# One decode step of attention and a gated feed-forward on one core: Gate's weights loaded in pieces of 112, 8 and 8 rows

## The chip, the cores and the metric

The kernel runs on one core of a Trainium2 chip. The metric is the device time of one execution in microseconds (us), as a median over repeated executions. Profiles are one execution each, taken by the hardware profiler; TensorE is called PE there (PEld for its weight loads), VectorE DVE, ScalarE ACT, GpSimd POOL and SyncE SP (SPq where it issues transfers).

## What is computed

One token (a row of 640 numbers) goes through a block with conditioning: a layer norm with a scale and a shift, attention over a cache of 16384 positions in 32 heads of 128, a gate and a residual; then a second layer norm, a gated feed-forward of width 1728, a gate and a residual. The reference, cut:

```python
mod = (_silu(c) @ w_mod).reshape(c.shape[0], 6, 1, -1)     # sa, ca, ga, sb, cb, gb
h = _layernorm(x) * (1 + ca) + sa
x = x + ga * attention(h, A_k_cache, A_v_cache, A_wq, A_wo)
h = _layernorm(x) * (1 + cb) + sb
x = x + gb * ((_silu(h @ w_gate) * (h @ w_up)) @ w_down)
```

All arrays are bf16. The two caches are 128 MiB each; `w_gate` and `w_up` are 640 x 1728 and `w_down` is 1728 x 640, some 2.2 MB each.

## The kernel before, in words

The caches go through the core once. Heads are taken in pairs, sixteen of them (`NP`). K of a pair (8 MB) goes to one of the two halves of `kring`, V to `vbuf`. The scores are made on VectorE: it multiplies K by the query laid out over the partitions (lines 546 and 561) and folds the products (lines 550, 555 and 567); TensorE adds up the rest with the identity as weights (lines 537 and 575). Softmax runs on ScalarE (line 593), and TensorE multiplies V by the weights (line 493). In the last pair (lines 639 to 647) K comes in two pieces and V in four, so that the work behind the last bytes is short.

Nearly all transfers are issued by SyncE, in the order in which the program lists them, through the helper at line 80. Each is issued when the buffer that it overwrites is free. Towards the end the order is: K of the last pair, V of the last pair but one, the output projection `A_wo` (into the half of `kring` that is free by then), V of the last pair in four pieces, and then the weights of the feed-forward, into the other half of `kring` (`kb`): gate (`wg_v`), up in two pieces (`wu_v`), down in four (`wd_v`). These last seven all wait for one thing, `o_R[NP - 1]`, the last sum of the scores on TensorE (line 704), which ends at about 640 us. So all of them stand in the queue behind V's last pieces, and each engine that moves data takes its share of one after the other.

Gate's load (line 705) is a single one. `w_gate` is laid out so that partition p holds five consecutive rows of the matrix: 5 x 1728 x 2 = 17280 bytes in a partition, one packet of the trace each, 128 in all. Here "row" means such a packet: the share of one partition. A load of 128 rows is moved by sixteen DMA engines, eight rows each, and each engine adds to the load's semaphore when its share has landed.

What uses these weights, on TensorE in this order: `gate0` (line 761) multiplies the first fifth of the gate matrix by `ab`, which VectorE makes from the second layer norm (line 759); then come the sum for the variance (line 381), the rest of gate (line 767), the residual as rows (`x1_rows`, line 780), `up0` and `up1` (lines 782 and 783) and, when VectorE has made `gu` (line 791) from both, the four parts of the down projection, `down0` to `down3` (line 805, matmuls at line 802). Each of the four waits for its own load (wd0 to wd3), and wd3 has only 96 rows, of 2560 bytes. VectorE then applies the last gate and the residual (lines 806 and 807), and the output is stored.

In the plan, every operation has a list of those that it depends on (`deps`), every load a semaphore of its own, and an engine waits for each semaphore with one instruction of its own ahead of the operation (lines 133 to 138).

Of the kernel before, what the change touches and what calls it, by code (L numbers as in the profile page):

```python
# [37 lines left out]
class _Plan:  # L38
# [28 lines left out]
    def op(self, eng, fn, deps=(), name="", chan=None):  # L67
        o = _Op(eng, fn, list(deps), name, len(self.ops), self.loop.get(eng), chan)
        o.sig = chan is not None
        self.ops.append(o)  # L70
        return o

    def dma(self, out_ap, in_ap, key, deps=(), name="", eng="sp", noncontig=False):
        nc = self.nc

        def fn(e, out_ap=out_ap, in_ap=in_ap, noncontig=noncontig):
            if noncontig:
                with nc.allow_non_contiguous_dma(reason="tiny vector layout change"):
                    return e.dma_start(out_ap, in_ap)
            return e.dma_start(out_ap, in_ap)  # L80

        return self.op(eng, fn, deps, name, chan=self.dma_chan(key))
# [125 lines left out]
def build(nc, A_x, A_k, A_v, A_wq, A_wo, B_wg, B_wu, B_wd, c_in, w_mod, out):  # L208
# [21 lines left out]
    with es:  # L230
        block = es.enter_context(nc.Block())
        plan = _Plan(nc, es)
        op, dma = plan.op, plan.dma
        POOL, ACT, DVE, PE = "pool", "act", "dve", "pe"
# [12 lines left out]
        wg_v = kb[:, 0:KC * F].rearrange("p (k n) -> p k n", k=KC)  # L247
# [68 lines left out]
        g_ps = psb[0]  # L316
# [53 lines left out]
        def layernorm_ops(src_f32, src_dep, sum_ap, c0, tag, xc_t, free=None, between=None):  # L370
            st_ps = misc
            o_tot = op(PE, lambda e: e.matmul(st_ps[:, c0:c0 + 1], lhsT=ones_f[:], rhs=sum_ap, start=True, stop=True),
                       deps=[src_dep, o_onesf, free], name=tag + "_tot")
            o_xc = op(DVE, lambda e: e.scalar_tensor_tensor(
                out=xc_t[:], in0=src_f32[:], scalar=float(D), in1=st_ps[:, c0:c0 + 1].broadcast_to([128, KC]),
                op0=ALU.mult, op1=ALU.subtract), deps=[o_tot, src_dep], name=tag + "_xc")
            o_sq = op(ACT, lambda e: e.activation(
                out=junk[:], in_=xc_t[:], func=ACTF.Square, accum_out=st[:, c0 + 1:c0 + 2]), deps=[o_xc], name=tag + "_sq")
            if between:
                between(o_xc)  # L380
            o_tot2 = op(PE, lambda e: e.matmul(st_ps[:, c0 + 1:c0 + 2], lhsT=ones_f[:], rhs=st[:, c0 + 1:c0 + 2], start=True, stop=True),
                        deps=[o_sq], name=tag + "_tot2")
            o_ln = op(ACT, lambda e: e.activation(
                out=st[:, c0 + 2:c0 + 3], in_=st_ps[:, c0 + 1:c0 + 2], func=ACTF.Ln, scale=1.0 / float(D) ** 3, bias=EPS),
                deps=[o_tot2], name=tag + "_ln")
            o_rstd = op(ACT, lambda e: e.activation(
                out=st[:, c0 + 3:c0 + 4], in_=st[:, c0 + 2:c0 + 3], func=ACTF.Exp, scale=-0.5, bias=-math.log(float(D))),
                deps=[o_ln], name=tag + "_rstd")
            return o_xc, o_rstd
# [20 lines left out]
        def f_mod(e, m0, m1):  # L410
# [11 lines left out]
            deps=[o_mod, o_xn], name="t1")  # L422
# [23 lines left out]
        for g in range(H // 4):  # L446
            b = g % 2
# [9 lines left out]
            for half in range(2):  # L457
# [4 lines left out]
                    deps=[o_q[g]], name="qbc%d_%d" % (g, half)))  # L462
# [54 lines left out]
        def diag_last():  # L517

            p, last = NP - 1, o_diag[NP - 2]
            copies = [op(ACT, lambda e, h=h: e.activation(  # L520
                out=acc_sb[:, 256 * h:256 * h + 256], in_=acc_ps[:, 256 * h:256 * h + 256], func=ACTF.Copy),
                deps=[o_pv[p], last], name="acc%d_%d" % (p, h)) for h in range(2)]
            for h in range(2):
                def f_diag(e, h=h):
                    out = None
                    for i in (2 * h, 2 * h + 1):
                        out = e.matmul(OT_ps[:, 0:2], lhsT=acc_sb[:, 128 * i:128 * (i + 1)], rhs=sel[:, i:8:4],  # L527
                                       start=(i == 0), stop=(i == 3))
                    return out
                o_diag[p] = op(PE, f_diag, deps=[copies[h], o_sel, o_ot[p - 1]], name="diag%d_%d" % (p, h))  # L530
            return o_diag[p]
# [89 lines left out]
        a = 0  # L621
        while a < len(GROUPS):
            b = a
            while b < len(GROUPS) and GROUPS[b][1] == GROUPS[a][1]:
                b += 1
            (h0, n), h1 = GROUPS[a], GROUPS[b - 1][0] + GROUPS[b - 1][1]
            d = dma(wo_v[:, h0:h1, :].rearrange("p (g k) n -> p g (k n)", k=n),
                    A_wo[h0 * 128:h1 * 128, :].rearrange("(g p k) n -> p g (k n)", p=128, k=n),
                    ("wo", a), deps=[o_R[NP - 2]], name="dma_wo%d" % a)
            for i in range(a, b):  # L630
                d_wo[i] = d
            a = b
# [12 lines left out]
                  deps=[o_exp[PL - 1], o_rz, o_onesf, o_rstd], name="La")  # L645
# [4 lines left out]
                  deps=[o_rla] + o_ot[0:NP - 1], name="on")  # L650
# [31 lines left out]
        def project(g):  # L682
            h0, n = GROUPS[g]

            def f_wo(e):
                last = None
                for k in range(h0, h0 + n):
# [11 lines left out]
                  deps=[o_exp[PL], o_rla], name="Lb")  # L699
# [2 lines left out]


        wdeps = [o_R[NP - 1]]
        d_wg = dma(wg_v, B_wg.rearrange("(p k) n -> p k n", p=128), "wg", deps=wdeps, name="dma_wg")
        wu_src = B_wu.rearrange("(p k) n -> p k n", p=128)
        UK = KC - 1
        d_wu = [dma(wu_v[:, 0:UK, :], wu_src[:, 0:UK, :], "wu0", deps=wdeps, name="dma_wu0"),
# [10 lines left out]
        for g in range(NG):  # L719
# [3 lines left out]
                   deps=[o_rl, diag_last()], name="on_last")  # L723

        def f_wol(e):
# [10 lines left out]
        o_zg = op(DVE, lambda e: e.memset(g_ps[:, 0:2 * FCH], 0.0), deps=[o_exp[NP - 2]], name="zero_g")  # L736
# [5 lines left out]
            deps=[o_ga, o_xf], name="x1")  # L742

        def chunk(j):
            return (slice(512 * (j // 4) + j % 4, 512 * (j // 4) + 512, 4), 128) if j < 4 * NB else (slice(512 * NB + j % 4, F, 2), FR)

        def f_gu(e, wv, ps_t, src, n, k0, k1):
            last = None
            for k in range(k0, k1):
                for j in range(FCH):  # L750
                    cols, w = chunk(j)
                    last = e.matmul(ps_t[0:w, n * j:n * j + n], lhsT=wv[:, k, cols], rhs=src[:, n * k:n * k + n],
                                    start=(k == 0 and j == 0), stop=(k == KC - 1 and j == FCH - 1), skip_group_check=True)
            return last
        ab_f = ab[:].rearrange("p k n -> p (k n)")
        o_g0 = []

        def gate0(o_xc1):
            o_a = op(DVE, lambda e: e.tensor_tensor(out=ab[:, :, 0], in0=xc1[:], in1=onep_b[:], op=ALU.mult),
                     deps=[o_xc1, o_onep_b, o_abs], name="ab_a")  # L760
            o_g0.append(op(PE, lambda e: f_gu(e, wg_v, g_ps, ab_f, 2, 0, 1), deps=[o_a, d_wg, o_zg], name="gate0"))
        o_xc1, o_rstd1 = layernorm_ops(x1, o_x1, st[:, 4:5], 4, "ln2", xc1, o_rl, gate0)
        o_t2 = op(DVE, lambda e: e.scalar_tensor_tensor(
            out=tt3[:], in0=xc1[:], scalar=st[:, 7:8], in1=onep_b[:], op0=ALU.mult, op1=ALU.mult),
            deps=[o_xc1, o_rstd1, o_onep_b], name="t2")
# [48 lines left out]
def bass_adaLN_cond__gqa_block_cached__swiglu_ffn__decode_kernel(  # L814
    nc: bass.Bass,
    A_x: bass.AP,
    A_k_cache: bass.AP,
    A_v_cache: bass.AP,
    A_wq: bass.AP,
    A_wo: bass.AP,  # L820
    B_x: bass.AP,
    B_w_gate: bass.AP,
    B_w_up: bass.AP,
    B_w_down: bass.AP,
    c: bass.AP,
    w_mod: bass.AP,
    out: bass.AP,
):
    build(nc, A_x, A_k_cache, A_v_cache, A_wq, A_wo, B_w_gate, B_w_up, B_w_down, c, w_mod, out)
# [28 lines left out]
```

## Time and profile before

| What | Value |
|---|---|
| median of 3 runs | 682.11 us (682.03 to 682.45) |
| the profiled execution: time | 682.26 us |
| the profiled execution: span of the profile | 680.5 us |
| data moved | 290.63 MB, mean 427 GB/s over the span |
| VectorE busy | 512.4 us (75%) |
| TensorE busy | 372.1 us (55%) |
| gate's load: issue, from issue to landing | 640.62 us, 25.2 us |
| down's loads: issue, from issue to landing | 641.94 us on, 30.6 to 33.5 us |

The span begins with the first instruction and ends with the last; the profiled execution's time holds 1.8 us more around it. Start times below are in us from the span's start. A line of the timeline gives start, duration, engine, line of the program, operation, what is written and read, the number of instructions and, in brackets, how long the engine had been idle and what released it. The chain of waits is followed back from the last instruction: each piece is what released the one after it. Beside instructions and packets, the trace keeps the time of every addition to a semaphore, and so of the sixteen arrivals of each load, though not the name of the engine that made one.

### The profile page before, as it was taken

Reading aid. Unit: us, or ns where it says so; the run is one execution under the profiler, and the core shown is the slowest. Engines: PE = TensorE matmul, PEld = TensorE weight load, DVE = VectorE, ACT = ScalarE, POOL = GpSimd, SP = SyncE. Lnnn points to the kernel's source line nnn. Section 1 sums busy time; section 2 is a strip of 40 time slices with the busy share of each in tenths; the row PEclk is TensorE's granted clock in tenths of the full one; section 3 lists DMA queues with packets and bytes.
Section 4 is the critical chain, followed back from the end, with each engine's and each line's share of the span. In section 5 each row is a group of like instructions: output and inputs, shape, how many; then the busy total and the mean of one; then the engine's idle time right before and its main releaser. Section 6 shows DMA issues by size and latency. Waiting matters only on the chain.

```text
span 680.5 us, 5104 instructions
## 1 busy us (share of the span) xinstructions
PE 372.1 (55%) x2271; PEld 151.9 (22%) x2272; DVE 512.4 (75%) x191; ACT 46.0 (7%) x146; POOL 0.7 (0%) x6
## 2 busy tenths in 40 slices
PE   2532275756638184655728275664817375572866
PEld 2311122221212122221302122221202122131435
DVE  2079998959596986959597895959598795999402
ACT  1120000100000000100000000000000010000100
POOL 0000000000000000000000000000000000000000
PEclk9975565655756565565657565565757555575665
DMA  8999999999999999999999999999999999999996
GB/s 369 443 460 429 431 431 428 432 432 431 431 431 431 431 435 431 435 431 435 431 431 431 431 447 443 439 435 435 431 431 431 431 431 431 410 453 403 436 414 271
DMA packets 7575, 290.63 MB, mean 427 GB/s; under 512 B 810, under 2 KB 1068, under 8 KB 2060
## 3 DMA queue, kind: packets, MB, share of 16 engines
q1 hardware_dynamic: 7560, 290.48, 99.1%
q8 instruction: 8, 0.13, 0.1%
q14 instruction: 3, 0.02, 0.0%
q10 hardware_dynamic: 4, 0.00, 0.0%
HBM read 290.47 MB, written 0.00 MB: 427 GB/s over the span
## 4 chain that ended last, share of the span: by engine, by line
DMA 54%; DVE 35%; PE 10%; SPq 0%; issue 0%; ACT 0%
DMA kring<-in_A_k_cache_dram 44%; DVE kring L546 17%; DVE kring L550 8%; PE psb L537 7%; DMA kring<-in_B_w_down_dram 5%; DMA vbuf<-in_A_v_cache_dram 4%; DVE kring L555 4%; DVE kring L561 3%; DVE kring L567 2%; PE psb L493 2%; PE psb L575 1%; SPq L80 0%; DVE pm L581 0%; PE psb L802 0%; PE psb L510 0%
## 5 line engine op out<-in xcount | busy, mean ns | idle before, releaser
L546 DVE TENSOR_TENSOR kring<-kring,qbc 128x16384 bf16<-128x16384 bf16 x28 | 243.3, 8688 | 95.1 <-DMA kring<-in_A_k_cache_dram 95.1
L537 PE MATMUL psb<-kring,ident 128*128 128x256 bf16 x448 | 197.4, 607 | 118.6 <-DVE kring L555 118.6
L550 DVE TENSOR_TENSOR kring<-kring 128x8192 bf16<-128x8192 bf16 x28 | 123.8, 4420 | 0.5
L537 PEld LDWEIGHTS psb<-kring,ident 128*128 128x128 bf16 x448 | 51.8, 121 | 248.5 <-DVE kring L555 128.3
L493 PE MATMUL psb<-vbuf,PZ 128*8 128x512 bf16 x1024 | 90.1, 526 | 11.4 <-DMA vbuf<-in_A_v_cache_dram 11.3
L585 PE MATMUL psb<-d,bd_f 128*128 128x64 f32 x32 | 11.0, 447 | 113.8 <-ACT d L583 113.8
L555 DVE TENSOR_TENSOR kring<-kring 128x4096 bf16<-128x4096 bf16 x28 | 64.0, 2286 | 0.5
L561 DVE TENSOR_TENSOR kring<-kring,qbc 128x16384 bf16<-128x16384 bf16 x4 | 34.7, 8687 | 17.0 <-DMA kring<-in_A_k_cache_dram 17.0
L493 PEld LDWEIGHTS psb<-vbuf,PZ 128*8 128x8 bf16 x1024 | 28.5, 109 | 77.2 <-issue 61.7
L585 PEld LDWEIGHTS psb<-d,bd_f 128*128 128x128 f32 x32 | 8.0, 311 | 115.6 <-DVE pm L581 58.2
L575 PE MATMUL psb<-kring,ident 128*128 128x128 bf16 x64 | 14.5, 393 | 35.0 <-DVE kring L567 35.0
L567 DVE TENSOR_TENSOR kring<-kring 128x8192 bf16<-128x8192 bf16 (+2 forms) x12 | 31.7, 2645 | 0.3
L510 PEld LDWEIGHTS psb<-sel,acc_sb 128*128 128x128 f32 x120 | 27.5, 318 | 7.2 <-issue 4.3
L510 PE MATMUL psb<-sel,acc_sb 128*128 128x2 f32 x120 | 24.5, 326 | 0.7 <-ACT acc_sb L501 0.7
L501 ACT ACTIVATE acc_sb<-psb 128x512 f32<-128x512 f32 x15 | 9.0, 597 | 209.7 <-PE psb L493 209.7
L593 ACT ACTIVATE PZ<-psb,nb 64x256 bf16<-64x256 f32 x32 | 15.0, 469 | 63.0 <-DVE nb L589 62.8
L575 PEld LDWEIGHTS psb<-kring,ident 128*128 128x128 bf16 x64 | 7.5, 122 | 41.4 <-DVE kring L567 36.1
L452 PE MATMUL psb<-vbuf,h_col 128*128 128x512 bf16 x39 | 11.0, 453 | 7.9 <-DMA vbuf<-in_A_wq_dram 7.9
L722 DVE TENSOR_TENSOR A_sb<-psb,rl 128x2 bf16<-128x2 f32 x1 | 0.2, 159 | 19.7 <-PE psb L527 19.7
L583 ACT ACTIVATE d<-negid,pm 128x64 f32<-128x64 f32 x16 | 5.6, 348 | 138.3 <-DVE pm L581 138.0
L514 ACT ACTIVATE OT_sb<-psb 128x2 f32<-128x2 f32 x15 | 2.6, 172 | 153.1 <-PE psb L510 153.1
L581 DVE TENSOR_REDUCE pm<-psb 128x1 f32<-128x256 f32 x16 | 6.7, 418 | 1.8 <-PE psb L575 1.8
(103 smaller groups left out, 91.6 us busy)
## 6 DMA issues: line engine op xcount, KB each, us to landing
kring<-in_A_k_cache_dram SPq DMA_DIRECT2D x4, 4096.0 KB, 37.6
vbuf<-in_A_wq_dram SPq DMA_DIRECT2D x1, 5120.0 KB, 27.0
kring<-in_w_mod_dram SPq DMA_DIRECT2D x1, 4800.0 KB, 14.1
vbuf<-in_A_v_cache_dram SPq DMA_DIRECT2D x1, 4096.0 KB, 15.7
kring<-in_A_wo_dram SPq DMA_DIRECT2D x1, 3840.0 KB, 29.2
kring<-in_B_w_gate_dram SPq DMA_DIRECT2D x1, 2160.0 KB, 25.2
vbuf<-in_A_v_cache_dram SPq DMA_DIRECT2D x1, 2048.0 KB, 20.2
kring<-in_B_w_down_dram SPq DMA_DIRECT2D x3, 640.0 KB, 32.3
```

Of the source, the lines that this page charges most:

```text
L452: last = e.matmul(q_ps[b][:, 0:512], lhsT=h_col[:, k:k + 1].broadcast_to([128, 128]), rhs=wq_v[:, k, g * 512:(g + 1) * 512], start=(k == 0 ...
L493: last = e.matmul(acc_ps[32 * s:32 * s + 8, :], lhsT=PZ[:, p % 2, j, :], rhs=vbuf[:, 4 * j:4 * j + 4, :].rearrange("p t d -> p (t d)"), st ...
L510: last = e.matmul(OT_ps[:, 0:2], lhsT=acc_sb[:, 128 * i:128 * (i + 1)], rhs=sel[:, i:8:4], start=(i == 0), stop=(i == 3))
L537: last = e.matmul(S_ps[p % 2][:, 0:T2], lhsT=ident[:], rhs=kring[:, p % 2, :, d], start=(d == 0), stop=(d == QW + QR - 1))
L546: o_m = op(DVE, lambda e: e.tensor_tensor(out=kv4, in0=kv4, in1=q4, op=ALU.mult), deps=[d_k[p][-1]] + o_qev[p // 2], name="mult%d_%d" % (p ...
L550: o_f = op(DVE, lambda e: e.tensor_tensor(out=kv4[:, :, 0], in0=kv4[:, :, 0], in1=kv4[:, :, 1], op=ALU.add), deps=[o_m], name="fold%d_%d" ...
L555: return op(DVE, lambda e: e.tensor_tensor(out=lo[:, :, 0:QR], in0=lo[:, :, 0:QR], in1=lo[:, :, QR:QW], op=ALU.add), deps=[o_f], name="fol ...
L561: o = op(DVE, lambda e: e.tensor_tensor(out=kv, in0=kv, in1=qbc[:, p, :].unsqueeze(1).broadcast_to([128, KCUT[c + 1] - KCUT[c], 128]), op= ...
L567: o = op(DVE, lambda e, w=w: e.tensor_tensor(out=kv[:, :, 0:w], in0=kv[:, :, 0:w], in1=kv[:, :, w:2 * w], op=ALU.add), deps=[o], name="fol ...
L575: last = e.matmul(S_ps[p % 2][:, KCUT[c]:KCUT[c + 1]], lhsT=ident[:], rhs=kring[:, p % 2, KCUT[c]:KCUT[c + 1], d], start=(d == 0), stop=(d ...
L585: o_mx[p] = op(PE, lambda e: e.matmul(mx_ps[:, 0:64], lhsT=bd_f[:], rhs=d2[:], start=True, stop=True), deps=[o_d2, o_bd1, o_bd2, o_nb[p - ...
L593: o_exp[p] = op(ACT, lambda e, half=half, ps=ps: e.activation(out=PZ[ps, p % 2, :, 4 * half:4 * half + 4], in_=S_ps[p % 2][ps, 0:T2].rearr ...
```

## The change

The single load of gate's weights becomes three: rows 0 to 111, rows 112 to 119 and rows 120 to 127. They are issued one after the other at the place of the old one, each with a semaphore of its own, and `gate0` waits for all three. 112 rows are seven for each of sixteen engines; the two loads of eight rows are meant for one row on each of the lower eight engines, so that these move nine rows and the upper eight seven. The same bytes go to the same places.

```diff
         wdeps = [o_R[NP - 1]]
-        d_wg = dma(wg_v, B_wg.rearrange("(p k) n -> p k n", p=128), "wg", deps=wdeps, name="dma_wg")
+        wg_src = B_wg.rearrange("(p k) n -> p k n", p=128)
+        d_wg = [dma(wg_v[a:b], wg_src[a:b], ("wg", a), deps=wdeps, name="dma_wg%d" % a) for a, b in ((0, 112), (112, 120), (120, 128))]
         wu_src = B_wu.rearrange("(p k) n -> p k n", p=128)
...
-            o_g0.append(op(PE, lambda e: f_gu(e, wg_v, g_ps, ab_f, 2, 0, 1), deps=[o_a, d_wg, o_zg], name="gate0"))
+            o_g0.append(op(PE, lambda e: f_gu(e, wg_v, g_ps, ab_f, 2, 0, 1), deps=[o_a, o_zg] + d_wg, name="gate0"))
```

## Prediction

> **What bounds the kernel now.** I read the page first, then the windows of the last 40 us, the timeline of the end, the chain and the waits. From the page:
>
> ```profile
> span 680.5 us, 5104 instructions
> ...
> DMA  8999999999999999999999999999999999999996
> ...
> q8 instruction: 8, 0.13, 0.1%
> q14 instruction: 3, 0.02, 0.0%
> ```
>
> The transfers are busy from the second slice to the last but one: the kernel moves 290.63 MB at a mean of 427 GB/s and waits for little else. The two last lines look idle, but they matter below: code loads of 16 KB and 8 KB run on the same sixteen DMA engines. The windows of the tail (columns: busy time of PE, PEld, DVE, ACT and POOL, then PEclk, DMA share, GB/s):
>
> ```profile
> 660.00:665.00 5.00, 3.95 (x34) 2.38 (x22) 0.30 (x4) 0.66 (x2) 0.00 (x0) 0.50 1.00 429
> 665.00:670.00 5.00, 3.96 (x78) 3.86 (x82) 1.78 (x11) 0.67 (x4) 0.00 (x0) 0.50 0.97 406
> 670.00:675.00 5.00, 4.36 (x98) 3.37 (x99) 1.17 (x6) 0.41 (x2) 0.00 (x0) 0.50 0.93 353
> 675.00:680.50 5.50, 1.82 (x40) 0.83 (x40) 0.65 (x2) 0.00 (x0) 0.00 (x0) 0.50 0.09 34
> ```
>
> The rate falls to 353 GB/s in 670 to 675: some engines run dry while others still work. What ends last, from the timeline:
>
> ```profile
> 674.12 0.70 PE L802 MATMUL psb<-kring,gu_col 128*1 128x160 bf16 x16 [0.33 <-DVE gu_col L791]
> 674.99 0.70 PE L802 MATMUL psb<-kring,gu_col 128*1 128x160 bf16 x16 [0.16 <-PE psb L802]
> 676.43 0.70 PE L802 MATMUL psb<-kring,gu_col 128*1 128x160 bf16 x16 [0.74 <-DMA kring<-in_B_w_down_dram]
> 677.30 0.43 PE L802 MATMUL psb<-kring,gu_col 96*1 96x160 bf16 x8 [0.17 <-PE psb L802]
> ```
>
> and from the chain of waits:
>
> ```profile
> 642.88 33.50 DMA kring<-in_B_w_down_dram
> 676.39 0.04 issue
> 676.43 0.73 PE psb L802 x14
> 677.16 0.14 issue
> 677.30 0.47 PE psb L802 x6
> ```
>
> The third of the four down projections (down2) starts 0.04 us after its weights land at 676.39; the fourth's land at 676.89 and it starts when PE is free. So the end of the kernel is the last arrival of W_down's third load plus 1.3 us of PE and 2.8 us behind it.
>
> A load of 128 rows adds to its semaphore sixteen times, once from each engine, and the trace keeps the events. I sorted them (us):
>
> ```
> load (bytes a row)       sixteen arrivals
> wg, gate (17280)         663.75 663.77 663.80 663.88 663.92 663.95 663.99 664.14 | 664.86 664.99 665.39 665.41 665.42 665.52 665.57 665.77
> wd0 (5120)               670.45 670.48 670.49 670.59 670.62 670.66 670.71 670.87 | 671.69 672.12 672.14 672.15 672.23 672.29 672.51 672.56
> wd2 (5120)               673.62 673.68 673.78 673.82 673.97 674.13 674.14 | 675.25 675.49 675.60 675.61 675.67 675.69 675.73 676.27 676.39
> wd3 (2560, 96 rows)      674.47 674.61 674.69 674.80 674.86 674.94 675.11 | 675.74 676.08 676.15 676.18 676.32 676.36 676.41 676.56 676.89
> ```
>
> At wg there are exactly eight early engines (within 0.39 us) and eight late ones (1.11 to 2.02 us behind). At the first load they lay within 0.53 us (14.34 to 14.87). Each step between is a code load: one of 16 KB at 21.86 us took 0.96 us, and one engine then arrived 1.87 us after the first; six such before wg, and two of 8 KB, made eight late engines, each another one. The seventh of 16 KB, at 671.77, turns an early engine into the 675.25 of wd2. Mean and last arrival of wd2 differ by 676.39 - 674.93 = 1.46 us: no even spread could gain more.
>
> **The change, part by part.**
>
> *Rows.* The trace's packets show wg's rows as one packet of 17280 bytes each, end to end on an engine, median 644 ns. Now an engine moves eight. 112 rows over sixteen are seven; each load of 8 rows is one row on each of eight engines. So eight engines get +0.644 us and eight -0.644 us, and the loads behind (up, down) inherit it, as they queue without a gap. That 112 rows split over all sixteen is read from wd3: 96 rows, sixteen arrivals, six rows each. That a short load takes as many engines as it has rows is read from the output's store: four rows, four packets within 679.74 to 679.80.
>
> *Two more loads.* Between two queued loads the trace shows one packet of 4 bytes, 9 ns, and the next row 6 ns after its start: 0.01 us for both on the eight lower engines. From above, the nearest row is a transfer with nothing ahead of it, the output's: issued 678.50, last arrival 680.14, 1.64 us. wu1 is nearer (432 KB queued behind wu0): its mean arrival is 1.11 us after wu0's against 8 x 0.135 = 1.08 us of packets. I take 0.01, and keep 2 x 1.64 = 3.3 for a rival. [...] The wu1 row does not agree with a fixed cost once loads queue.
>
> *Rows on other engines than before.* Seven rows an engine cut the partitions at other places than eight. wd3, cut in sixes, has rows of 2560 bytes at a median of 102 ns; the 128-row load of the same row size (output projection, heads 28 and 29) also has 102. I take zero, from zero to 0.2 us.
>
> *Issue on SP.* The wg issue took 0.33 us, the next two 0.91 together; two more put up and down about 0.9 us later in SP's queue, at 641 to 643 us. Their data run from 664 on, so 20 us of queue hide it; SP already stands 12 us in one W_down issue because the queue is full. Nothing else is behind them on SP but the output's store at 678.50. If that cover were gone, it would be 0.9 us.
>
> *Waits on PE.* gate0 now waits for three semaphores. It starts at 666.63, 0.06 us after ab_a; wg's last arrival is 665.77, or 666.42 if it slips 0.65, still earlier. Two passed waits more on PE: the nearest row, the step from down0 to down1 with its wait already met, has about 0.16 us idle, so 0 to 0.3 us for both, on PE's compute chain. Behind gate0 on PE stand the variance sum, gate, x1 rows, up and down. That chain ends with down0 at 674.12. Run without waits, the 56 matmuls (16 in 0.70 us) take 2.45 us, so PE alone would end at 676.6 rather than 677.73: 1.1 us of cover. That is also the most that any balance of engines can gain.
>
> *The sum, if the late eight are the eight that get seven rows.* wd2: the last late arrival goes to 676.39 - 0.64 = 675.75; the early engine that took the code load at 671.77 goes to 675.25 + 0.65 = 675.90 and is now last: -0.49. wd3: 676.89 - 0.64 = 676.25 against 675.74 + 0.65 = 676.39: -0.50. Down2 starts 0.49 us earlier, at 675.94, and the end follows. The profiled execution took 682.26 (span 680.5 and 1.8 around it): 681.77. It lies 0.15 above the median of 682.11, so **681.6** against the median.
>
> **Which eight are late** decides the sign, and arrivals carry no engine's name. For the upper eight: the bunches are eight and eight; code loads fell on a different engine each time, which looks like dealing in turn, and a turn gives neighbours. [...]
>
> **Rivals.**
> 1. *The late bunch is, wholly or by its last engine, among those with nine rows* (27 in 100). Then the last arrival of wd2 slips by 0.644 + 0.01: down2 at 677.08, and 682.26 + 0.65 = 682.9 profiled, 682.8 by the median. It is slower from the point where one late engine of the last three (676.27, 676.39 or the like) has nine rows; if only an engine of the middle (675.7) has, it is +0.0.
> 2. *The end does not follow* (8 in 100): the slow packets around 673.5 to 674.3 us (5120 bytes in 230 to 430 ns instead of 196) come at a fixed time and hold whichever engines are left. Then the gain shrinks to 0 to 0.2: 682.1.
> 3. *The split loads pay a price of their own* (7 in 100), or 112 rows do not go over all sixteen. With 1.64 us a load: 682.1 + 3.3 = 685.4; with fourteen rows on eight engines, six more rows of 0.644, 3.9 us: 686. [...]
>
> **How the numbers follow.** The forecast has 58 in 100: 681.6, itself from 681.3 (all 0.64 and a little of the slow packets) to 681.9. With rivals 1 and 2, 93 in 100 lie in 681.3 to 682.9, and leaving out less would need rival 3, so that is the range. A measurement of this kernel can tell about 0.2% (1.4 us) from no change; the gain's cap of 1.1 us and rival 1's 0.65 are both inside it. Faster by more: 0.02, for what I have not seen; slower by more: 0.07, rival 3; same: 0.91.
>
> **What would show it.** Sixteen arrivals on the 112-row load and eight on each small one; at wu0 the two bunches closing from 1.1-2.0 us apart to overlapping (right) or opening to 1.3 more (rival 1); down2 starting near 675.9, 677.1 or 676.4; gate0 still released by ab_a. Small loads arriving over 1 us after the 112-row one on the same engines would be rival 3. What makes it wrong most easily is the naming of the engines.

## The result, and the profile after

The changed kernel takes 690.29 us (median of 4 runs, 689.79 to 690.85) against 682.23 (4 runs, 682.03 to 682.45): 1.0118 times as long, 95% interval 1.0105 to 1.0130. It is 8.1 us slower; I had said 681.6, at most 682.9. Its profiled execution took 690.77 us with a span of 689.0.

The same windows of the tail as before (PE, PEld, DVE, ACT and POOL, then PEclk, DMA share, GB/s), of the changed kernel:

```profile
655.00:660.00 5.00, 1.04 (x16) 0.30 (x16) 0.00 (x0) 0.00 (x0) 0.00 (x0) 0.80 1.02 350
660.00:665.00 5.00, 2.89 (x20) 1.18 (x21) 0.00 (x0) 0.66 (x2) 0.00 (x0) 0.50 1.09 251
665.00:670.00 5.00, 2.17 (x17) 1.92 (x17) 1.09 (x9) 0.30 (x2) 0.00 (x0) 0.50 0.98 181
670.00:675.00 5.00, 1.15 (x22) 1.18 (x23) 0.00 (x0) 0.00 (x0) 0.00 (x0) 0.50 0.94 273
675.00:680.00 5.00, 4.68 (x110) 4.06 (x109) 1.99 (x10) 0.78 (x4) 0.00 (x0) 0.50 0.99 407
```

Read the last two columns together. The DMA engines are as busy as before (0.94 to 1.09), but from 660 to 675 they move 251, 181 and 273 GB/s where they had moved 429, 406 and 353. Busy is time in which a packet is under way, not bytes. Then the timeline of PE in the changed kernel: gate's first matmuls, the third down projection and the fourth:

```profile
673.85 0.70 PE L753 MATMUL psb<-ab,kring 128*128 128x2 bf16 x14 [5.69 <-DMA kring<-in_B_w_gate_dram]
684.86 0.70 PE L803 MATMUL psb<-kring,gu_col 128*1 128x160 bf16 x16 [1.08 <-DMA kring<-in_B_w_down_dram]
685.72 0.44 PE L803 MATMUL psb<-kring,gu_col 96*1 96x160 bf16 x8 [0.16 <-PE psb L803]
```

In the kernel before, gate's first matmuls were released by VectorE:

```profile
666.63 0.73 PE L752 MATMUL psb<-ab,kring 128*128 128x2 bf16 x14 [0.46 <-DVE ab L759]
```

Now they wait 5.69 us for gate's weights. And the chain of waits still ends in W_down's third load and the two matmul groups behind it:

```profile
646.89 37.92 DMA kring<-in_B_w_down_dram
684.82 0.04 issue
684.86 0.73 PE psb L803 x14
685.59 0.14 issue
685.72 0.47 PE psb L803 x8
```

So the end is of the same kind as before, 8.4 us later in this execution. The time was lost in gate's loads. A row of 17280 bytes, one packet, took a median of 644 ns before; in the changed kernel the fastest of the 128 takes 804 ns, the median 1226 and the longest 1841. The arrivals (us):

```
112 rows        667.03 667.18 667.20 667.32 667.51 667.53 667.60 667.70 669.84 669.89 670.22 670.67 670.97 671.08 672.66 672.76
8 rows, first   641.53 | 668.40 668.80 668.97 669.08 671.63 671.93 671.99 672.12
8 rows, second  641.90 | 670.21 670.58 670.64 671.14 673.14 673.19 673.28 673.72
```

The 112 rows do go over sixteen engines. A load of eight rows has eight arrivals and one entry at its issue. And the second line answers what arrivals before could not: of the eight engines with nine rows, four follow the early bunch of the first line and four the late one. The second small load's arrivals come, in order, 1.26 to 2.06 us after the first's, about the time of a row here, which fits the same eight engines. No trace numbers the engines: "lower" stands for those that take the loads of eight rows, "upper" for the others.

### The profile page after: what moved, and what is told of

The parts are those of the page before. It is cut to its first block, busy times and chain, and to the rows that moved or that the text cites. A ratio compares the mean times of both kernels' runs of the same rounds, so it can differ in the third digit from the quotient of the medians.

```text
span 689.0 us, 5108 instructions
## 1 busy us (share of the span) xinstructions
PE 368.6 (54%) x2272; PEld 151.3 (22%) x2272; DVE 512.4 (74%) x191; ACT 46.0 (7%) x146; POOL 0.7 (0%) x6
## 4 chain that ended last, share of the span: by engine, by line
DMA 54%; DVE 34%; PE 10%; SPq 1%; issue 0%; ACT 0%
DMA kring<-in_A_k_cache_dram 44%; DVE kring L546 16%; DVE kring L550 8%; PE psb L537 7%; DMA kring<-in_B_w_down_dram 6%; DMA vbuf<-in_A_v_cache_dram 4%; DVE kring L555 4%; DVE kring L561 3%; DVE kring L567 2%; PE psb L493 2%; PE psb L575 1%; SPq L80 1%; DVE pm L581 0%; PE psb L803 0%; PE psb L510 0%
## 5 line engine op out<-in xcount | busy, mean ns | idle before, releaser
L493 PE MATMUL psb<-vbuf,PZ 128*8 128x512 bf16 x1024 | 86.4, 509 | 13.4 <-DMA vbuf<-in_A_v_cache_dram 13.4
```

Source lines behind the costliest of these rows:

```text
L493: last = e.matmul(acc_ps[32 * s:32 * s + 8, :], lhsT=PZ[:, p % 2, j, :], rhs=vbuf[:, 4 * j:4 * j + 4, :].rearrange("p t d -> p (t d)"), st ...
```

## Experiments

The theories: **P**, the rows of such a load are dealt so that engines meet in the same groups of partitions and slow each other; **F**, each further load has a price; **A**, the places in memory that are read at once are bad; **I**, the unevenness itself, nine rows for late engines. Beside each run's median stands that of the kernel before, measured together with it. The diffs are cut: they show lines that differ from the kernel before, and where gate's load has become a list, `wg_src` is that of the first diff and `gate0` waits for the whole list, as in the change. Packet times are medians unless a mean is named. Four medians (112 and 16 rows, 64 and 64, 96 and 32, and the loads side by side) rest on two executions each.

**Three loads, cut by columns.**

```diff
+        wg_src = B_wg.rearrange("(p k) n -> p k n", p=128)
+        d_wg = [dma(wg_v[:, a:b], wg_src[:, a:b], ("wg", a), deps=wdeps, name="dma_wg%d" % a) for a, b in ((0, 3), (3, 4), (4, 5))]
```

> Gate's weights in three loads as in the change, but cut by columns: all 128 rows in each, 3, 1 and 1 fifths of a row. Every engine keeps eight rows of the same partitions, and PE waits for three semaphores. Theory P (rows dealt to engines in sevens meet in the same groups of partitions and slow each other): nothing of that is here, 682.1 to 682.4, row packets at the old rate (10368 bytes in about 390 ns). Theory F (each further load pays a price): two further loads as in the change, so some 690. Theory A (the places in memory that sixteen engines read at once) as P: 682.

Measured: 682.30 against 682.27, ratio 1.000 (0.9989 to 1.0012); packets of 10368 bytes take 389 ns. F falls, and with it any cost of the issues on SP and the waits on PE.

**112 and 16 rows**, eight an engine again.

```diff
+        d_wg = [dma(wg_v[a:b], wg_src[a:b], ("wg", a), deps=wdeps, name="dma_wg%d" % a) for a, b in ((0, 112), (112, 128))]
```

> Gate's weights in two loads of 112 and 16 rows: every engine has eight rows again, so nothing is uneven, and one load more instead of two. P: the 112 rows are cut in sevens as in the change, so their packets stay near 1200 ns instead of 644 and the time is 688 to 691. F: half of the 8.1 us, 686. Theory I (nine rows on engines that are late): no unevenness, 682.2.

Measured: 689.26 (688.75 and 689.76) against 682.27, 1.0103 (1.0074 to 1.0132); packets of 17280 bytes with a median of 1287 ns. Of the 8.1 us, 7.0 are there without any unevenness.

**64 and 64 rows.**

```diff
+        d_wg = [dma(wg_v[a:b], wg_src[a:b], ("wg", a), deps=wdeps, name="dma_wg%d" % a) for a, b in ((0, 64), (64, 128))]
```

> Gate's weights in two loads of 64 rows, four on each engine, no unevenness. P: 64 partitions at a time take the bytes that 128 took, so packets of 17280 bytes go from 644 to about 1290 ns and the eight rows of an engine need some 5.2 us more: 686 to 688. F: one load more, 686, but packets of 644 ns. I: 682.2. [...]

Measured: 689.60 against 682.27, 1.0108 (1.0079 to 1.0137), more than I expected. The mean arrivals say where: gate's two loads need 5.28 and 5.22 us, 10.5 together, where one needed 5.13 (+5.4, as expected); but V's last piece ahead of them lands 1.0 us later on the mean, and up's first load behind takes 4.97 instead of 4.09. So the loads on both sides slow down too, and I had left these seams out. That it is the early engines, already in the slow load, which hold up late ones in the load ahead, and the other way round at its end, fits this but is argued: no packet names its engine.

**Other places in memory, same partitions.** 128 rows of 15120 bytes and 128 of 2160; the weights lie otherwise over the partitions, so the numbers of the output are not the reference's.

```diff
+        wg_f, wg_s = kb[:, 0:KC * F], B_wg.rearrange("k n -> (k n)")
+        NA, NT = 7 * KC * F // 8, KC * F
+        d_wg = [dma(wg_f[:, 0:NA], wg_s[0:128 * NA].rearrange("(p n) -> p n", p=128), ("wg", 0), deps=wdeps, name="dma_wg0"),
+                dma(wg_f[:, NA:NT], wg_s[128 * NA:128 * NT].rearrange("(p n) -> p n", p=128), ("wg", 1), deps=wdeps, name="dma_wg1")]
```

> Gate's weights as 128 rows of 15120 bytes and 128 of 2160 (the same bytes of memory, but laid over the partitions otherwise, so that the numbers of the output are not the reference's). [...] P: 682.2, packets of 15120 bytes in about 565 ns. [...]

Measured: 682.39 against 682.27, 1.0002 (0.9991 to 1.0013); packets of 15120 bytes take 565 ns. So this spacing of the rows in memory costs nothing. It doesn't settle A, since no trace names which engine reads which row, and so the run can't show that it read the places of the cut loads; the loads into free space, further down, change the partitions and leave the places in memory as they are.

**Even and odd partitions**, 64 rows each, which tells the partitions apart from the number of rows.

```diff
+        d_wg = [dma(wg_v[a:128:2], wg_src[a:128:2], ("wg", a), deps=wdeps, name="dma_wg%d" % a) for a in (0, 1)]
```

> Gate's weights in two loads of 64 rows, as the run with 64 and 64 (689.6), but one has the even partitions and the other the odd ones, so that each load is spread over all 128. If a load is slow only because 64 neighbouring partitions offer half of the paths, the time is 682.2 to 683 and packets take 644 ns. [...]

Measured: 682.26 against 682.23, 0.9999 (0.9989 to 1.001). Its packet counts between 658 and 672 us, then those of the run with 64 and 64 neighbouring rows, then those of the kernel before:

```profile
DMA packets 786, 5.91 MB, mean 422 GB/s; under 512 B 108, under 2 KB 108, under 8 KB 523
```

```profile
DMA packets 293, 3.10 MB, mean 222 GB/s; under 512 B 52, under 2 KB 52, under 8 KB 120
```

```profile
DMA packets 773, 5.94 MB, mean 424 GB/s; under 512 B 93, under 2 KB 93, under 8 KB 508
```

Two loads of 64 rows of the same size, at the same place of the queue: 422 GB/s when they are spread over all partitions, 222 when they fill one half at a time. The two runs also read other rows of memory together, which the loads into free space below don't. Taken with those, the runs show the part of P that lies in the partitions: which of them are filled at one time decides the rate. How the rows are dealt to the engines is not shown.

**96 and 32 rows**, the cut of W_down's last load on large rows.

```diff
+        d_wg = [dma(wg_v[a:b], wg_src[a:b], ("wg", a), deps=wdeps, name="dma_wg%d" % a) for a, b in ((0, 96), (96, 128))]
```

> Gate's weights in two loads of 96 rows (six an engine, as W_down's last load, which my prediction took as the proof that a cut in sixes costs nothing) and 32 (two an engine). No engine has more than eight rows. P: with rows of 17280 bytes and six of them, the engines are all inside the load together, packets go to 1000 to 1300 ns and the time is 687 to 690; W_down's last load of six rows of 102 ns hid that because it is shorter (0.6 us) than the engines lie apart (2.4 us). If a cut in sixes really costs nothing, 32 rows alone are slow: 1.3 to 2.6 us, 683.5 to 685.

Measured: 689.09 against 682.23, 1.010 (1.008 to 1.0121); median packet 1221 ns. By mean arrivals the load of 96 rows took 7.44 us, where six undisturbed rows are 3.86, so it isn't the 32 rows alone: a cut in sixes is as bad as one in sevens (689.09 against 689.26).

**Four more loads for the lower eight engines**, into free space, their partitions four apart; then the same with the partitions side by side.

```diff
+        FREE = 2 * KC * F + FCH * D
+        wg_rows = B_wg.rearrange("(p k) n -> p (k n)", p=128)
+        d_sp = [dma(kb[i:32:4, FREE:T2 * 128], wg_rows[8 * i:8 * i + 8, 0:T2 * 128 - FREE], ("spare", i), deps=wdeps, name="dma_spare%d" % i) for i in range(4)]
...
-        d_sp = [dma(kb[i:32:4, FREE:T2 * 128], wg_rows[8 * i:8 * i + 8, 0:T2 * 128 - FREE], ("spare", i), deps=wdeps, name="dma_spare%d" % i) for i in range(4)]
+        d_sp = [dma(kb[8 * i:8 * i + 8, FREE:T2 * 128], wg_rows[8 * i:8 * i + 8, 0:T2 * 128 - FREE], ("spare", i), deps=wdeps, name="dma_spare%d" % i) for i in range(4)]
```

> Gate's load is the single one of before. Behind it stand four further loads of eight rows of 13056 bytes into free space of the same partitions, which nothing reads: work on the lower eight engines alone, four rows each, with the eight partitions of a load four apart (0, 4, ... 28, then 1, 5, ...). [...] Theory I: if some of the late engines are among the lower eight, the end moves by 1.0 to 1.95 us, to 683.2 to 684.2; if all late ones are upper (as my prediction had it), by 0 to 0.5. Theory F: 8 to 16 us.

> As the kernel with the four further loads four partitions apart, with the same 32 rows of memory read in the same order and the same 32 partitions written, but each load writes eight partitions side by side (0 to 7, 8 to 15, ...). [...] A and I: as the other, 682.2 to 684.2, with packets of 487 ns.

Measured: 684.49 (1.0033, 1.0021 to 1.0046) and 686.59 (1.0064, 1.0044 to 1.0084) against 682.23. Four apart, packets take 488 ns (13056 bytes at the rate of 17280 in 644 ns would be 487, an estimate) and the end moves by 2.26 us for 1.95 us of work (four packets an engine), a little more than I expected; the eight arrivals of the first of these loads (664.16 to 664.42, four; 664.89 to 665.85, four) again show four early engines and four late. So the unevenness is real, some 1.16 us of time for each us; by the same ratio the change's 0.644 would cost 0.75, an estimate. Side by side, with the same bytes, the same rows of memory in the same order and the same 32 partitions in all, the median packet is 800 ns. Only the partitions that a load fills together differ, so for these loads A falls. The time is above the 682.2 to 684.2 of A and I. Why a packet takes 800 ns and not some other time, no run shows.

**Nine and seven without the cut**, and its control with four even loads.

```diff
+        d_wg = [dma(wg_v[a:b:4], wg_src[a:b:4], ("wg", a), deps=wdeps, name="dma_wg%d" % a) for a, b in ((0, 128), (1, 128), (2, 128), (3, 32), (35, 64), (67, 128))]
...
+        d_wg = [dma(wg_v[a:b:4], wg_src[a:b:4], ("wg", a), deps=wdeps, name="dma_wg%d" % a) for a, b in ((0, 128), (1, 128), (2, 128), (3, 128))]
```

> The change's division without its cut: gate's rows in three loads of 32 rows, every fourth partition of all 128 (two rows an engine each), two loads of eight rows, every fourth partition below 64, for the lower eight engines, and one of sixteen rows, every fourth partition from 64 on. The lower engines have nine rows and the upper seven, as in the change, in six loads. Theory P with the unevenness beside it: packets stay near 644 ns but for the last sixteen (up to 1290), and the lower engines end 0.64 us later than before; the four 8-row loads into free space showed four late engines among them, so the end slips by about 0.65: 682.7 to 683.4. If nine and seven themselves cost the 8 us: 690. If the late engines are the upper ones: 681.6.

> Gate's rows in four loads of 32 rows, every fourth partition: two rows an engine and load, eight in all, no unevenness. Theory P: packets of 644 ns, 682.1 to 682.5. If a load of fewer than 128 rows is slow whatever partitions it has (32 side by side took 2 to 3 times in the run with 96 and 32): 687 and more. If each load has a price: 683 and more.

Measured: 684.34 (1.003, 1.0018 to 1.0043) and 682.19 (1.000, 0.999 to 1.001) against 682.22. The control is clean: 32 rows of all partitions cost nothing, packets of 644 ns. Nine and seven cost 2.1, not 0.65: from 663.1 us on, when the last loads of eight and sixteen rows and then up's are under way, packets are slow (up's mean 645 ns instead of 516). The run confirms that the cut makes most of the 8 us, but it did not isolate the unevenness; the four loads into free space do.

**The cut on a fifth of the bytes**, to see why W_down's last load had shown nothing.

```diff
+        d_wg = [dma(wg_v[a:b, k:m], wg_src[a:b, k:m], ("wg", i), deps=wdeps, name="dma_wg%d" % i)
+                for i, (a, b, k, m) in enumerate(((0, 128, 0, 4), (0, 112, 4, 5), (112, 128, 4, 5)))]
```

> Four fifths of each of gate's rows in one load of 128 rows, and the last fifth (3456 bytes a row) in loads of 112 and 16 rows: the cut in sevens on a fifth of the bytes, with eight rows an engine as before. The question is why W_down's last load, 96 rows of 2560 bytes, showed hardly any of the slowness. If the slowness goes with the bytes that are cut: a fifth of the 7.0 us of the run with 112 and 16 rows, 1.4 us, 683.6, with packets of 3456 bytes at 230 to 270 ns instead of 135. If a short load hides it, because its share on an engine (0.95 us) is shorter than the engines lie apart (2.0 us) and few are inside it together: less than 0.5 us, 682.2 to 682.7, with most packets at 135.

Measured: 684.37 against 682.15, 1.0034 (1.0021 to 1.0047). The median packet of the cut fifth is 212 ns, not the undisturbed 135 (I had said 230 to 270), and the loads on both sides slow too. So a short load did not hide the slowness here; it cost 2.2 us, more than its share of 1.4.

**W_down's last load moved ahead of up's.** (`FR` is its 96 rows, `NB` its number, 3.)

```diff
+        d_wd3 = dma(wd_v[0:FR, 4 * NB:FCH, :].rearrange("p r n -> p (r n)"),
+                        B_wd[512 * NB:F, :].rearrange("(p r) n -> p (r n)", r=2), ("wd", NB), deps=wdeps, name="dma_wd%d" % NB)
         wu_src = B_wu.rearrange("(p k) n -> p k n", p=128)
...
-        d_wd.append(dma(wd_v[0:FR, 4 * NB:FCH, :].rearrange("p r n -> p (r n)"),
-                        B_wd[512 * NB:F, :].rearrange("(p r) n -> p (r n)", r=2), ("wd", NB), deps=wdeps, name="dma_wd%d" % NB))
+        d_wd.append(d_wd3)
```

> Gate's load is the single one of before. Only W_down's last load (96 rows of 2560 bytes, six an engine) is moved: it is issued right behind gate's, ahead of up's, instead of at the end of the queue. It asks why this load showed hardly any slowness in the kernel before (packets of 102 ns, a mean of 112). If that was its place, last in the queue with nothing behind it to be met: packets with a mean of 150 to 200 ns, rows of up's load slowed at the seam, and 682.8 to 683.5. If it was the small row or the small burst (15 KB an engine): packets near 102 ns and 681.7 to 682.3; with wd2 then the last to land, PE's last part no longer waits for a transfer of its own.

Measured: 683.54 against 682.34, 1.0017 (1.0008 to 1.0027). In the middle of the queue the same 96 rows take a mean of 141 ns, just under the 150 to 200 that I gave, and the neighbours slow (up's first load 644 ns instead of 516). And at the end of the queue, where the load had been, the slow packets of 5120 bytes are gone: 2 of 384 over 225 ns, against 30 before.

**W_down's last load on all 128 partitions**, at its old place.

```diff
-        d_wd.append(dma(wd_v[0:FR, 4 * NB:FCH, :].rearrange("p r n -> p (r n)"),
-                        B_wd[512 * NB:F, :].rearrange("(p r) n -> p (r n)", r=2), ("wd", NB), deps=wdeps, name="dma_wd%d" % NB))
+        d_wd.append(dma(wd_v[:, 4 * NB:FCH, :].rearrange("p r n -> p (r n)"),
+                        B_wd[F - 256:F, :].rearrange("(p r) n -> p (r n)", r=2), ("wd", NB), deps=wdeps, name="dma_wd%d" % NB))
...
-            return (slice(512 * (j // 4) + j % 4, 512 * (j // 4) + 512, 4), 128) if j < 4 * NB else (slice(512 * NB + j % 4, F, 2), FR)
+            return (slice(512 * (j // 4) + j % 4, 512 * (j // 4) + 512, 4), 128) if j < 4 * NB else (slice(F - 256 + j % 4, F, 2), 128)
...
+        o_gz = op(DVE, lambda e: e.memset(gu_col[0:128 - FR, 4 * NB:FCH], 0.0), deps=[o_gum], name="gu_twice")
...
-            prev = op(PE, f_down, deps=[o_gum, d_wd[b], prev, o_fz], name="down%d" % b)
+            prev = op(PE, f_down, deps=[o_gum, d_wd[b], prev, o_fz] + ([o_gz] if b == NB else []), name="down%d" % b)
```

> Gate's load is the single one of before. W_down's last load stays last, but has 128 rows of 2560 bytes instead of 96 (the last 256 rows of the matrix; the 32 partitions that come twice get a zero factor, one small VectorE write beside down0). If the slow packets at 673.5 to 674.3 us (5120 bytes in 230 to 430 ns instead of 196) are engines of the 96-row load meeting late engines that still move wd2: they go to 196 to 210, wd2's last arrival comes 0.2 to 0.5 us earlier, and the time is 681.7 to 682.0 in spite of two more rows of 102 ns an engine. If they are an event at a fixed time: they stay, and the time is 682.2 to 682.5.

Measured: 681.60 (11 runs, 681.42 to 681.72) against 682.24, 0.999 (0.9981 to 0.9999): the fastest of all and a little below the 681.7 that I gave, with more bytes to move. Its timeline (down2, the fourth part, and the small write beside down0):

```profile
673.14 0.06 DVE L792 MEMSET gu_col<- 32x1 uint32 x1
...
675.75 0.70 PE L803 MATMUL psb<-kring,gu_col 128*1 128x160 bf16 x16 [0.85 <-DMA kring<-in_B_w_down_dram]
...
676.62 0.43 PE L803 MATMUL psb<-kring,gu_col 128*1 128x160 bf16 x8 [0.17 <-PE psb L803]
```

down2 starts 0.68 us earlier than before (676.43). All 128 packets of the last load take 102 to 114 ns, and 3 of the 384 of 5120 bytes take over 225. The gain is 0.64 us. Moved or spread, the load leaves no slow packets behind at the end, so those of the kernel before came from its 96 rows and not from an event at a fixed time.

## Why the prediction was wrong

**The step that failed** is "Rows on other engines than before", where I took zero, from zero to 0.2 us. It measured 7.0 us (112 and 16 rows). I had read the zero from the median of W_down's last load, the undisturbed 102 ns. But ten of its 96 packets took over 150, and most of its cost fell on other packets, the rows of 5120 bytes still under way in the load ahead of it: 30 of 384 took over 225 ns. I had seen these slow packets and made them rival 2, something that comes at a fixed time. They were the one sign of the mechanism in the trace of before; moving or spreading that load takes them away. So the range was too narrow as well: the one load that was not cut in eights had a disturbance beside it, and that was the price to bound.

**Which eight are late.** I gave the late bunch to the upper eight. No trace of before shows which engines a load of eight rows takes; that they would be the early ones was my guess, and the -0.49 of the sum rests on it. Of the eight engines that got nine rows, four are early and four late (668.40 to 669.08 and 671.63 to 672.12 us), so rival 1's mechanism held beside the main one. Its price, 0.65, is about 0.75 by the loads into free space. Added up, which no run tests, cut and unevenness (7.0 and 0.75) make 7.8 of the 8.1 us. The other 0.3 needs no cause of its own: the runs of the changed kernel alone lie 1.1 us apart, and those with 112 and 16 rows 1.0.

**Rival 3** came nearest in time, for a reason that falls: two further loads cost nothing (682.30), and the 112 rows go over all sixteen engines.

**What held.** The load's sixteen arrivals and eight for each small one; 0.01 us for two more loads; the issues on SP and the waits on PE hidden (three loads and three waits by columns: 682.30; SP's first long issue is W_down's fourth load before, 12.06 us, and its second load after, 3.73, each the eleventh issue from the one at 635.15 or 635.18 us on, which fits a queue that is full); the end set by W_down's third load. That gate0 stays released by VectorE did not hold: the 0.85 us of cover were far too little. The cap of 1.1 us on what balance can gain was not tried.

**Open** is the dealing itself. Eight undisturbed rows are 5.15 us, an estimate from eight packets of 644 ns; the seven of the 112-row load took 8.9 (mean arrival 660.26 to 669.20). Which engine is given which partition, and when, may be the cause; no run here shows that order. For 64 rows it is shown that the partitions filled together set the rate (422 against 222 GB/s), for 112 and 96 only that the cut is what costs.

## What to carry to other kernels

Cut a load by columns (682.30 us here), or by every second or fourth partition (682.26 and 682.19), so that each piece is still spread evenly over all 128 partitions; pieces of 64, 96 or 112 neighbouring partitions ran at about half the rate here (222 GB/s with 64 and 64 rows, 226 with 112 and 16, against 424 in the same window of before; packets of 1221 ns against 644 with 96 and 32), and slowed the loads queued on either side (with 64 and 64, V's last piece landed 1.0 us later and up's first load took 4.97 us instead of 4.09). When you judge a resource, set its busy share beside its bytes per second: the engines were 94 to 109% busy at 181 to 273 GB/s. And when a trace holds one instance of what a change will do on a larger scale, look at the whole spread of its packets and at its neighbours, not at the median.

## What the runs showed that I had not expected

A load slows the one ahead of it: V's last piece, ahead of gate's, had packets of 4096 bytes with a mean of 235 ns instead of 163 when gate came as 64 and 64 rows, although the slow load stood behind it. And a load of 96 rows at the very end of the kernel, 240 KB of 290 MB, held back the end by 0.6 us.
